# Columns 16 to 31 summed on VectorE and transposed by DMA; softmax sums of the later batches by accumulating transfers

## The chip, the cores and the metric

The kernel runs on one core of a Trainium2 chip. The metric is the device time in microseconds (us) of one execution. A core has five engines that run their own instruction streams in order: TensorE (PE, matrix products, with PEld for its weight loads), VectorE (DVE), ScalarE (ACT), GpSimd (POOL) and SyncE (SP). The last two mainly issue DMA transfers here. An instruction that has to wait holds up whatever stands behind it in the stream of its engine; between engines only semaphores order the work.

## The reference

Two stages. The first is a dynamic convolution: each position s of a batch has, for each of H = 8 heads, K = 7 weights, normalised by a softmax, which weigh the last 7 positions of x (D = 192 channels, 24 to a head). The second is a two-layer network whose hidden layer takes the maximum of two products.

```python
w = exp(weight_gen - max(weight_gen));  w = w / sum(w)        # [8, 4160, 8, 7], over the 7 taps
out[b,s,h,:] = sum over k of w[b,s,h,k] * x_padded[b, s+k, h, :]
y = out.reshape(33280, 192)
result = maximum(y @ w1, y @ w2) @ w_out                      # w1, w2: 192x1024, w_out: 1024x192
```

## The kernel before, in words

**Tiling.** The 33280 positions lie 260 to a partition on 128 partitions. One "column" is one position on every partition. Columns are taken in 17 batches: 16 of 16 columns and one of 4 (`BATCHES`, L50). `pieces` (L54) cuts a batch into units that are multiplied and summed at once: four units of 4 columns in batches 0 and 1, two of 8 columns in batches 2 to 15, one of 4 in the last. I write (b, o) for the unit of batch b that begins at its column o. PE works through 260 tiles, one a column's worth of hidden layer, in groups: 8 groups of two tiles (tiles 0 to 15), then groups of three (`GROUPS`, L71). Tiles 16 to 31 are batch 1, tile 32 begins batch 2.

**The softmax of a batch.** `load_wg` loads its weights (POOL queue). ACT takes the exponential (`exp_sum`, L131), DVE sums over the 7 taps (`red`, L143), ACT takes the logarithm (`ln`, L149), DVE subtracts it from the raw weights (`shift`, L153, in three pieces), and ACT takes the exponential of that, doubled and reordered by tap, as bf16 weights `en_t` (`weights`, L159), one call for each unit.

**The convolution.** DVE multiplies the unit's x by `en_t` for all seven taps into `m_t` (`mul`, L173), then adds the taps in three instructions (`adds`, L188: 3 pairs, 2 pairs, the last one into `y_t`). `transpose` (L212) issues a transposing DMA on SP's queue from `y_t` to `yt`, and then puts on POOL a "gate": a one-element copy that reads `yt` (L224) and so waits for the transfer. Behind the gate on POOL stand the next loads of x, a copy of six columns from one x tile to the next (`load_halo`, L123), and, for a unit at o = 0, the weights of batch b + 3.

**Batches 0 and 1 are different.** PE itself adds the taps there: `sum_transpose` (L239) multiplies `m_t` by an identity, accumulating over the taps, which sums and transposes in one, and ACT copies the result to `yt` (L255). In batch 0 DVE adds nothing. In batch 1 DVE makes the first of the three adds for the units at 4, 8 and 12 (`adds(..., True)`), so that four "taps" are left (`LEFT`); for the unit at 0 PE adds all seven.

**The network.** For each tile `hid_tile` (L291) makes the hidden products in PSUM, with w2 - w1 in place of both; ACT applies a relu (`relu`, L306); `out_first` and `out_second` (L345, L361) multiply by `w_out` and add the w1 part by a product with w1 @ w_out made once. ACT copies the output from PSUM (`evac`, L377), and SP stores it. A group with output columns has a relay on ACT (`relay`, L370) between the two halves of its output products, so PE waits there for ACT.

**Order.** All orders are written out by hand (`manual_schedule`). `hidden` (L458) makes one group: hidden products, output products of earlier columns, relus, the relay, the output copy. Up to group 7 the softmax and DVE steps stand explicitly in the code (L561 to L719: `rest_of_1`, `end_of_1`, and the table `early` with what goes into groups 3 to 7). From tile 16 on the table `due` (L721) says at which tile a softmax step of batch c is put into ACT's and DVE's order, and `extra` (L748) places `mul`, `adds` and `transpose` of the batches ahead: at tile 0 of batch b stands `mul(b + 1, 0)`, at tile 8 `mul(b + 1, 8)`, and the subtraction of batch b + 2 and the reduction of batch b + 3 run between the adds. `behind` (L262) gives a load one more thing to wait for, so that it takes its place among the transfers. How many columns of output each group takes (`OUTS`, L426) follows from which tiles are complete at its start, up to 4.

Of the kernel before, what the change touches and what calls it, by code (L numbers as in the profile page):

```python
# [9 lines left out]
FP32 = mybir.dt.float32  # L10
BF16 = mybir.dt.bfloat16
I32 = mybir.dt.int32
AF = mybir.ActivationFunctionType
# [10 lines left out]
def kernel(  # L24
# [9 lines left out]
    nc = tc.nc  # L34
# [19 lines left out]
    def pieces(b):  # L54
        n = BATCHES[b][1]
        at, done = [], 0
        for w in (4, 4, 4, 4) if b < 2 else (8, 8) if n == 16 else (n,):
            at.append((done, w))
            done += w
        return at  # L60
# [70 lines left out]
    def exp_sum(b, i=0, of=1):  # L131
        if i == 0:
            e_ts[b] = pe_.tile([P, BATCHES[b][1] * WGC], FP32, name="e_t", tag="e")
        w = BATCHES[b][1] * WGC // of
        nc.scalar.activation(out=e_ts[b][:, i * w:(i + 1) * w], in_=wg_ts[b][:, i * w:(i + 1) * w], func=AF.Exp)  # L135

# [6 lines left out]
    def red(b, i=0, of=1):  # L143
        if i == 0:
            s_ts[b] = psm.tile([P, BATCHES[b][1] * H], FP32, name="sum_t", tag="sum")
        hs, at, ap = part(b, i, of)
        nc.vector.reduce_sum(out=s_ts[b][:, hs], in_=_sub(e_ts[b], at, ap), axis=AX.X)  # L147

    def ln(b, i=0, of=1):  # L149
        s_t = s_ts[b][:, part(b, i, of)[0]]  # L150
        nc.scalar.activation(out=s_t, in_=s_t, func=AF.Ln)
# [7 lines left out]
    def weights(b, o):  # L159

        w = dict(pieces(b))[o]
        if b not in en_ts:
            en_ts[b] = pen.tile([P, 16 * WGC * 2], BF16, name="en_t", tag="en")
        J = 2 if w == 4 and b < 2 else 1
        N = w * H // J
        for j in range(J):
            nc.scalar.activation(  # L167
                out=_sub(en_ts[b], (o * WGC + j * N * K) * 2, [[2 * N, K], [2, N], [1, 2]]),
                in_=_sub(wg_ts[b], (o * H + j * N) * K, [[1, K], [K, N], [0, 2]]), func=AF.Exp,
            )  # L170


    def mul(b, o):  # L173

        n = dict(pieces(b))[o]
        if n == 4 and b < 2:
            m_out = _sub(m_t, K * o * D, [[64, 2], [P, K * 6], [1, 64]])
            x_in = _sub(xb_ts[b], o * D, [[2 * D, 2], [D, K], [1, 2 * D]])
        else:
            m_out = m_t[:, K * o * D:K * (o + n) * D]  # L180
            x_in = _sub(xb_ts[b], o * D, [[D, K], [1, n * D]])
# [6 lines left out]
    def adds(b, o, first=False, beside=lambda i, of: None):  # L188
# [10 lines left out]
        if first:  # L199
            return  # L200
# [11 lines left out]
    def transpose(u):  # L212
# [17 lines left out]
        if o == 0 and b + 3 < NB:  # L230
            load_wg(b + 3, nc.gpsimd)
# [5 lines left out]
    LEFT = (0, 1, 2, K - 1)  # L237

    def sum_transpose(u, taps=range(K)):  # L239
# [4 lines left out]
        for k in range(6):  # L244
            for t in taps:
                for r in range(2):
# [4 lines left out]
                        start=(k == 0 and t == taps[0]), stop=(t == taps[-1]),  # L251
# [260 lines left out]
    with tc.tile_pool(name="pstage", bufs=1) as pstage:  # L512
# [173 lines left out]
        weights(1, 4)  # L686
        mul(1, 4)
        relu(rd, 7, 1)
        exp_sum(2)
        red(2)  # L690
        adds(1, 4, True)
# [7 lines left out]
    def rest_of_1():  # L699
        mul(1, 8)  # L700

    def end_of_1():
        shift(2)
        adds(1, 8, True)
        mul(1, 12)
        exp_sum(3)
        red(3)
        adds(1, 12, True)


    none = lambda: None
    early = {
        3: (none, rest_of_1),
        4: (lambda: (behind(relu_of[8], load_x(2, 0, 8, halo=False)), sum_transpose(4),
                     behind(yt_of[4], load_wg(4, nc.gpsimd))), end_of_1),
        5: (lambda: sum_transpose(5, LEFT), none),
        6: (lambda: (behind(relu_of[12], load_x(2, 8, 8)), weights(2, 8), ln(3), sum_transpose(6, LEFT)), none),
        7: (lambda: (behind(relu_of[14], load_x(3, 0, 8)), sum_transpose(7, LEFT)), none),
# [3 lines left out]
    for c in range(3, NB):  # L722
        soon = c < 8
        parts_ = [(16 * (c - 2) + (8 if soon else 10 if c < NB - 1 else 15), True, lambda c=c: weights(c, 0))]
        if 8 in dict(pieces(c)):
            parts_.append((16 * (c - 2) + (14 if soon else 15), True, lambda c=c: weights(c, 8)))
        if c > 3:
            ln_at = -2 if c == 4 else 0 if c < 8 else 2 if c < 11 else 4
            parts_.append((16 * (c - 2) + ln_at, False, lambda c=c: ln(c)))
            parts_.append((16 * (c - 3) + (4 if c < 8 else 7), True, lambda c=c: exp_sum(c)))  # L730
# [17 lines left out]
    def extra(t):  # L748
# [7 lines left out]
        later = 0 if b < 4 else 5  # L756
        if s == later and b + 1 < NB:

            c = b + 1
            adds(c, 0, beside=lambda i, of: shift(c + 1, i, of) if c + 1 < NB else None)  # L760
        if s == 8 and b + 2 < NB:
            mul(b + 1, 8)
        if s == 8 + later and b + 2 < NB:
            adds(b + 1, 8, beside=lambda i, of: red(b + 3, i, 2) if b + 3 < NB and i < 2 else None)
        if k == n // 4 - 1 and 7 < u + 1 < NU:
            transpose(u + 1)

# [11 lines left out]
    early[3][1]()  # L779
    for g in range(4, len(GROUPS)):  # L780
# [3 lines left out]
        if g in early:  # L784
            hidden(g, OUTS[g], early[g][0], ahead=lambda: {4: lambda: (weights(1, 12), ln(2)), 5: lambda: weights(2, 0)}.get(g, none)())
            early[g][1]()
            steps(g, tiles)
# [32 lines left out]
```

## Time and profile before

| | |
|---|---|
| runs | 413.61, 412.78, 410.75 us; median 412.78 |
| span of the profiled execution | 409.1 us, first to last instruction (no other time of that execution is given) |
| granted TensorE clock, mean | 0.997 |
| PE, DVE, ACT, POOL busy | 97%, 92%, 87%, 17% of the span |
| DMA moved | 65.68 MB, mean 161 GB/s |
| `mul`, 8 columns (L182) | 28 instructions, mean 5751 ns |
| `adds`, 8 columns (L198, L204, L207) | 28 each, mean 2551, 1751 and 955 ns |
| sums over taps (L147), half a batch | 26 instructions, mean 614 ns |
| PE's partial sums (L248) | 564 matmuls, 9.8 us busy |
| gate copy (L224) | 29, mean 1171 ns |

How to read it: the page counts an engine as busy while an instruction of it runs. Successive instructions of DVE and ACT overlap by 0.05 to 0.15 us, so that what an instruction costs its engine is the distance from its start to the next start, a little under its duration. In a row of a timeline the columns are start, length, engine, line, operation, output and inputs; a bracket at the end gives the idle time of the engine before it and what ended that. In a row of a group they are the count, busy time, mean duration in ns, and the idle time before them.

### The profile page before, as it was taken

The page shows a single profiled execution, that of the slowest core. Times are in us where ns is not written, and L with a number is a line of the kernel's source. Part 1 is how long each engine was busy: PE and PEld are TensorE (multiplying, and loading weights), DVE is VectorE, ACT ScalarE, POOL GpSimd, SP SyncE. Part 2 cuts the span into 40 slices and gives each one's busy share as a digit, 9 for nine tenths or more (in the row PEclk, how much of TensorE's full clock was granted, in tenths as well). Part 3 has the DMA queues.
Part 4 walks back from the last instruction along what each step waited for, and adds up shares of the span by engine and source line. Part 5 has one row for each costly group of instructions (what it writes and reads, how often), then busy time and mean ns, then how long its engine had stood idle before and what let it go on. Part 6 is the DMA issues. An engine that isn't in the chain of part 4 may idle for free.

```text
span 409.1 us, 15992 instructions
## 1 busy us (share of the span) xinstructions
PE 398.8 (97%) x7350; PEld 317.1 (78%) x7350; DVE 374.4 (92%) x219; ACT 357.4 (87%) x424; POOL 68.7 (17%) x101
## 2 busy tenths in 40 slices
PE   7999999999999999999999999999999999999995
PEld 2688999677777777777777777777787777787795
DVE  6999999999999999999999999999999999999000
ACT  6899989999999988999988999988999989888771
POOL 0321101222211021221101221210122212210000
PEclk9999999999999999999999999999999999999998
DMA  8966667658657874963796497489648648744513
GB/s 245 250 152 164 116 151 186 143 143 184 150 97 219 217 118 99 260 176 74 224 195 146 96 251 180 82 195 238 120 106 241 166 64 244 151 89 79 213 61 136
DMA packets 60384, 65.68 MB, mean 161 GB/s; under 512 B 47615, under 2 KB 48511, under 8 KB 60318
## 3 DMA queue, kind: packets, MB, share of 16 engines
q1 hardware_dynamic: 51934, 40.54, 36.0%
q0 software_dynamic: 8240, 24.04, 29.5%
q8 instruction: 57, 0.93, 0.9%
q10 hardware_dynamic: 144, 0.10, 0.1%
q14 instruction: 9, 0.07, 0.1%
HBM read 35.96 MB, written 25.56 MB: 150 GB/s over the span
## 4 chain that ended last, share of the span: by engine, by line
DVE 73%; PE 17%; issue 4%; DMA 4%; SPq 0%; DVEq 0%; ACT 0%
DVE m_t L182 37%; DVE m_t L198 15%; DVE m_t L204 10%; PE op_ps L339 9%; PE hd L299 7%; DVE sum_t L147 3%; DVE y_t L207 3%; DVE wg_t L156 3%; DMA xs<-in_x_dram 3%; PE op_ps L351 2%; DMA yt<-y_t 1%; DVE wd L582 0%; DVE xb_t L618 0%; SPq L521 0%; SPq L104 0%
## 5 line engine op out<-in xcount | busy, mean ns | idle before, releaser
L309 ACT ACTIVATE rd_t<-hd 128x1024 bf16<-128x1024 f32 (+1 forms) x206 | 234.6, 1189 | 28.0 <-PE hd L299 26.5
L339 PE MATMUL op_ps<-wo,rd_t 64*128 64x192 bf16 x4160 | 210.6, 243 | 0.1
L339 PEld LDWEIGHTS <-rd_t 64*128 64x128 bf16 x4160 | 180.8, 94 | 15.7 <-ACTq L372 0.3
L299 PE MATMUL hd<-yt,wd 64*128 64x512 bf16 (+1 forms) x1584 | 187.3, 360 | 1.4 <-ACT rd_t L309 1.2
L182 DVE TENSOR_TENSOR m_t<-xb_t,en_t 128x10752 bf16<-128x10752 bf16 (+1 forms) x37 | 187.4, 5071 | 0.2
L299 PEld LDWEIGHTS <-wd 64*128 64x128 bf16 x1776 | 94.1, 94 | 43.3 <-issue 3.3
L224 POOL CAST gate<-yt 128x1 f32<-128x1 bf16 x29 | 34.0, 1171 | 275.7 <-DMA yt<-y_t 275.7
L198 DVE TENSOR_TENSOR m_t<-m_t 128x4608 bf16<-128x4608 bf16 (+1 forms) x32 | 76.8, 2401 | 0.1
L395 ACT COPY o_t<-op_ps 128x384 f32<-128x384 f32 (+1 forms) x99 | 57.3, 591 | 13.4 <-PE op_ps L339 13.3
L351 PE MATMUL op_ps<-w,yt 64*128 64x192 bf16 x780 | 55.5, 243 | 1.1 <-ACT o_t L395 1.0
L351 PEld LDWEIGHTS <-yt 64*128 64x128 bf16 x780 | 38.4, 94 | 17.5 <-issue 2.1
L204 DVE TENSOR_TENSOR m_t<-m_t 128x3072 bf16<-128x3072 bf16 (+1 forms) x29 | 50.0, 1724 | 0.1
L167 ACT ACTIVATE en_t<-wg_t 128x896 bf16<-128x896 f32 (+2 forms) x45 | 35.3, 820 | 0.0
L207 DVE TENSOR_TENSOR y_t<-m_t 128x1536 bf16<-128x1536 bf16 (+1 forms) x29 | 27.3, 941 | 0.5
L385 DVE COPY o_last<-op_ps 128x192 f32<-128x192 f32 x1 | 0.4, 358 | 25.9 <-ACT o_last L385 25.9
L156 DVE TENSOR_TENSOR wg_t<-wg_t,sum_t 128x280 f32<-128x280 f32 (+5 forms) x46 | 22.0, 481 | 0.0
L147 DVE TENSOR_REDUCE sum_t<-e_t 128x64 f32<-128x448 f32 (+2 forms) x31 | 19.6, 636 | 2.6 <-ACT e_t L135 2.6
L114 POOL DMA_DIRECT2D xb_t<-in_x_dram x33 | 17.7, 535 | 23.3 <-ACT rd_t L309 11.8
L135 ACT ACTIVATE e_t<-wg_t 128x896 f32<-128x896 f32 (+2 forms) x18 | 16.1, 899 | 2.5 <-DMA wg_t<-in_weight_gen_dram 2.5
L309 ACT ACTIVATE rd_t<-hdp 128x1024 bf16<-128x1024 f32 x16 | 16.2, 1048 | 0.6 <-PE hdp L299 0.6
L613 PE MATMUL warm<-ident 128*128 128x512 bf16 x38 | 11.0, 457 | 2.6 <-DVE ident L560 2.6
L299 PE MATMUL hdp<-yt,wd 64*128 64x256 bf16 x192 | 12.9, 269 | 0.1
(46 smaller groups left out, 73.6 us busy)
## 6 DMA issues: line engine op xcount, KB each, us to landing
out_dram<-o_t SPq DMA_DIRECT2D x28, 768.0 KB, 5.0
xb_t<-in_x_dram POOLq DMA_DIRECT2D x30, 384.0 KB, 5.2
wg_t<-in_weight_gen_dram POOLq DMA_DIRECT2D x14, 448.0 KB, 5.2
xb_t<-xb_t POOLq DMA_DIRECT2D x16, 288.0 KB, 5.2
out_dram<-o_t SPq DMA_DIRECT2D x8, 384.0 KB, 2.9
wg_t<-in_weight_gen_dram SPq DMA_DIRECT2D x2, 448.0 KB, 4.5
xs<-in_x_dram SPq DMA_DIRECT2D x2, 384.0 KB, 6.0
xb_t<-in_x_dram POOLq DMA_DIRECT2D x3, 192.0 KB, 5.1
```

What stands on the lines that cost most here:

```text
L156: nc.vector.tensor_tensor(out=w_t, in0=w_t, in1=_sub(s_ts[b], hs.start, [[1, hs.stop - hs.start], [0, K]]), op=ALU.subtract)
L167: nc.scalar.activation(out=_sub(en_ts[b], (o * WGC + j * N * K) * 2, [[2 * N, K], [2, N], [1, 2]]), in_=_sub(wg_ts[b], (o * H + j * N) * K ...
L182: return nc.vector.tensor_tensor(out=m_out, in0=x_in, in1=_sub(en_ts[b], o * WGC * 2, [[2, K * n * H], [0, G // 2], [1, 2]]), op=ALU.mult,)
L198: nc.vector.tensor_tensor(out=taps(0, 1, 3), in0=taps(0, 1, 3), in1=taps(3, 1, 3), op=ALU.add)
L204: nc.vector.tensor_tensor(out=taps(0, 2, 2), in0=taps(0, 2, 2), in1=taps(1, 5, 2), op=ALU.add)
L207: nc.vector.tensor_tensor(out=_sub(y_ts[b], o * D, [[64, 2], [P, 3 * w // 2], [1, 64]]), in0=taps(0, 1, 1), in1=taps(2, 1, 1), op=ALU.add,)
L224: nc.gpsimd.tensor_copy(out=gate, in_=yt[:, 0:1])
L299: nc.tensor.matmul(hid_out(t, f, j), lhsT=wd_at(j, s, f // 4, f % 4 * P, P), rhs=_sub(yt_ts[u][half(j), :], (s + j) % 3 * P, [[3 * P, w // ...
L309: relu_of[t0] = nc.scalar.activation(out=rd[:, k * 1024:(k + n) * 1024], in_=hd[:, at:at + n * 1024], func=AF.Relu)
L339: return nc.tensor.matmul(op_out(c), lhsT=rd[half(r), k * 1024 + at:k * 1024 + at + P], rhs=wo[half(r), f * D:(f + 1) * D], start=False, s ...
L351: nc.tensor.matmul(op_out(c + j), lhsT=yt_ts[u][half(j), (3 * i + (s + j) % 3) * P:(3 * i + (s + j) % 3 + 1) * P], rhs=w10[half(j), s * D: ...
L395: nc.scalar.copy(out=_sub(o, c % 24 * D, [[D, len(qs)], [h * D, 2], [1, D]]), in_=_sub(tile_, at + (qs[0] - p) * D, [[D, len(qs)], [512, 2 ...
```

## The change

1. Batch 1 is cut into two units of 8 columns as the later batches are. DVE makes all three adds for them and the transposing DMA moves the result; PE's partial sums of batch 1, ACT's copies of them and `LEFT` go. In the order this puts `mul(1, 0)`, `adds(1, 0)` and the transfer of unit 4, (1, 0), before group 5, and `adds(1, 8)` behind group 4.
2. For batches 3 to 15 (`by_dma`) the exponential is written in seven planes, one a tap, and three accumulating DMAs on POOL's queue add them: planes 3 to 5 onto 0 to 2, then two onto two, then one onto one. Each must wait for the one before. ACT takes the logarithm from plane 0. DVE's reductions for these batches go. One accumulate is placed behind each gate; batch 3 has its three in a row behind group 4, batch 4 its three in a row behind the gate of unit 5.
3. The subtraction goes in six pieces over both halves' adds (`shifts`), in place of three.
4. The due tiles of the softmax steps move, and the weights of a batch are loaded behind the gate of batch b - 4 instead of b - 3. The weights of batch 4 are loaded in group 5's place, their exponential stands behind group 7.

As group 4 starts when only four units of batch 0 are ready in the new cut, it gets no output columns, and the groups after it take up its two, until from group 18 on the distribution is as before.

```diff
@@ pieces
-        for w in (4, 4, 4, 4) if b < 2 else (8, 8) if n == 16 else (n,):
+        for w in (4, 4, 4, 4) if b == 0 else (8, 8) if n == 16 else (n,):
@@ exp_sum, red, ln
+        if by_dma(b):
+            N = BATCHES[b][1] * H
+            nc.scalar.activation(out=_sub(e_ts[b], 0, [[1, N], [N, K]]), in_=_sub(wg_ts[b], 0, [[K, N], [1, K]]),
+                                 func=AF.Exp)
+            return
...
+    def by_dma(b):
+        return 3 <= b < NB - 1
+
+    def add_planes(b, step):
+        if not by_dma(b):
+            return
+        N, e_t = BATCHES[b][1] * H, e_ts[b]
+        to, frm = (((0, [[1, 3 * N]]), (3 * N, [[1, 3 * N]])),
+                   ((0, [[N, 2], [1, N]]), (2 * N, [[4 * N, 2], [1, N]])),
+                   ((0, [[1, N]]), (N, [[1, N]])))[step]
+        nc.gpsimd.dma_start(out=_sub(e_t, *to), in_=_sub(e_t, *frm), accum_op=ALU.add)
...
     def red(b, i=0, of=1):
+        if by_dma(b):
+            return
...
     def ln(b, i=0, of=1):
+        if by_dma(b):
+            N = BATCHES[b][1] * H
+            s_ts[b] = psm.tile([P, N], FP32, name="sum_t", tag="sum")
+            nc.scalar.activation(out=s_ts[b], in_=e_ts[b][:, 0:N], func=AF.Ln)
+            return
@@ transpose, behind the gate
-        if o == 0 and b + 3 < NB:
-            load_wg(b + 3, nc.gpsimd)
+        if o == 0 and b + 4 < NB:
+            load_wg(b + 4, nc.gpsimd)
+        if o == 0 and b + 2 > 4:
+            add_planes(b + 2, 2)
+        if o == 8 and b + 3 > 4:
+            add_planes(b + 3, 1)
+        if u == 5:
+            for i in range(3):
+                add_planes(4, i)
@@ the first groups
-        weights(1, 4)
-        mul(1, 4)
         relu(rd, 7, 1)
         exp_sum(2)
-        red(2)
-        adds(1, 4, True)
+        adds(1, 0, beside=lambda i, of: red(2, i, 2) if i < 2 else None)
         sum_transpose(3)
         weights(1, 8)
...
+    def after_4():
+        exp_sum(3)
+        for i in range(3):
+            add_planes(3, i)
+        transpose(4)
+        adds(1, 8, beside=lambda i, of: shift(2, i, 2) if i < 2 else None)
+
     early = {
...
+        4: (lambda: behind(relu_of[8], load_x(2, 0, 8, halo=False)), lambda: ln(2), after_4),
+        5: (lambda: behind(relu_of[10], load_wg(4, nc.gpsimd)), lambda: None, lambda: None),
+        7: (lambda: None, lambda: None, lambda: exp_sum(4)),
     }
@@ due tiles
+    for c in range(2, NB):
+        t0 = 16 * (c - 2)
+        if c == 2:
+            parts_ = [(16, True, lambda: weights(2, 0)), (20, True, lambda: weights(2, 8))]
+        else:
+            parts_ = [(t0 + (11 if c < NB - 1 else 15), True, lambda c=c: weights(c, 0)),
+                      (t0 + 3, False, lambda c=c: ln(c))]
+            if 8 in dict(pieces(c)):
+                parts_.append((t0 + 20, True, lambda c=c: weights(c, 8)))
+        if c > 4:
+            parts_.append((t0 - 22 if by_dma(c) else t0 - 14, True, lambda c=c: (exp_sum(c), add_planes(c, 0))))
@@ extra
+        if s == 5 and b + 1 < NB:
+            adds(b + 1, 0, beside=lambda i, of: shifts(b + 2, i))
...
+        if s == 13 and b + 2 < NB:
+            adds(b + 1, 8, beside=lambda i, of: (shifts(b + 2, 3 + i) if by_dma(b + 2) else None,
+                                                 red(b + 3, i, 2) if b + 3 < NB and i < 2 else None))
```

More of the change, by code (lines that the diff above doesn't have):

```diff
@@ L163, in weights @@
             en_ts[b] = pen.tile([P, 16 * WGC * 2], BF16, name="en_t", tag="en")
-        J = 2 if w == 4 and b < 2 else 1
+        J = 2 if b == 0 else 1
         N = w * H // J
@@ L175, in mul @@
         n = dict(pieces(b))[o]
-        if n == 4 and b < 2:
+        if b == 0:
             m_out = _sub(m_t, K * o * D, [[64, 2], [P, K * 6], [1, 64]])
@@ L186, in mul, with adds @@
         )
-    def adds(b, o, first=False, beside=lambda i, of: None):
+    def adds(b, o, beside=lambda i, of: None):
         w = dict(pieces(b))[o]
@@ L198, in adds @@
         nc.vector.tensor_tensor(out=taps(0, 1, 3), in0=taps(0, 1, 3), in1=taps(3, 1, 3), op=ALU.add)
-        if first:
-            return
         beside(1, 3)
@@ L229, in transpose, with sum_transpose @@
             load_x(c, 8, BATCHES[c][1] - 8)
-        if o == 0 and b + 3 < NB:
-            load_wg(b + 3, nc.gpsimd)
+        if o == 0 and b + 4 < NB:
[7 more added lines that the diff above has]
+                add_planes(4, i)
     def half(j):
         return slice(64 * j, 64 * j + 64)
-    LEFT = (0, 1, 2, K - 1)
-    def sum_transpose(u, taps=range(K)):
+    def sum_transpose(u):
         b, o, n = UNITS[u]
@@ L244, in sum_transpose @@
         for k in range(6):
-            for t in taps:
+            for t in range(K):
                 for r in range(2):
@@ L250, in sum_transpose @@
                         lhsT=m_t[half(r), at:at + P], rhs=ident[half(r), half(r)],
-                        start=(k == 0 and t == taps[0]), stop=(t == taps[-1]),
+                        start=(k == 0 and t == 0), stop=(t == K - 1),
                         skip_group_check=True,
@@ L696 @@
     o_t.append(pout.tile([P, 24 * D], FP32, name="o_t", tag="o"))
[L699 to L705, printed above, removed]
+    def after_4():
         exp_sum(3)
-        red(3)
-        adds(1, 12, True)
-    none = lambda: None
+        for i in range(3):
+            add_planes(3, i)
+        transpose(4)
+        adds(1, 8, beside=lambda i, of: shift(2, i, 2) if i < 2 else None)
     early = {
[L713 to L718, printed above, removed]
+        4: (lambda: behind(relu_of[8], load_x(2, 0, 8, halo=False)), lambda: ln(2), after_4),
+        5: (lambda: behind(relu_of[10], load_wg(4, nc.gpsimd)), lambda: None, lambda: None),
+        7: (lambda: None, lambda: None, lambda: exp_sum(4)),
     }
     due = {}
[L722 to L730, printed above, removed]
+    for c in range(2, NB):
[9 more added lines that the diff above has]
+            parts_.append((t0 - 22 if by_dma(c) else t0 - 14, True, lambda c=c: (exp_sum(c), add_planes(c, 0))))
         for t, *step in parts_:
@@ L755, in extra, with shifts @@
             mul(b + 1, 0)
[L756 to L760, printed above, removed]
+        if s == 5 and b + 1 < NB:
+            adds(b + 1, 0, beside=lambda i, of: shifts(b + 2, i))
         if s == 8 and b + 2 < NB:
             mul(b + 1, 8)
-        if s == 8 + later and b + 2 < NB:
-            adds(b + 1, 8, beside=lambda i, of: red(b + 3, i, 2) if b + 3 < NB and i < 2 else None)
-        if k == n // 4 - 1 and 7 < u + 1 < NU:
+        if s == 13 and b + 2 < NB:
+            adds(b + 1, 8, beside=lambda i, of: (shifts(b + 2, 3 + i) if by_dma(b + 2) else None,
+                                                 red(b + 3, i, 2) if b + 3 < NB and i < 2 else None))
+        if k == n // 4 - 1 and u + 1 < NU:
             transpose(u + 1)
+    def shifts(c, i):
+        if c < NB:
+            shift(c, i, 6 if by_dma(c) else 3)
     def steps(g, tiles):
@@ L778 @@
     evac(OUTS[3][0] // 2, len(OUTS[3]) // 2)
-    early[3][1]()
+    mul(1, 8)
     for g in range(4, len(GROUPS)):
@@ L784 @@
         if g in early:
-            hidden(g, OUTS[g], early[g][0], ahead=lambda: {4: lambda: (weights(1, 12), ln(2)), 5: lambda: weights(2, 0)}.get(g, none)())
-            early[g][1]()
-            steps(g, tiles)
+            between, ahead, after = early[g]
+            hidden(g, OUTS[g], between, ahead=ahead)
+            after()
         else:
```

## The prediction

> **What bounds the kernel now.** I read the busy shares first, then the chain that ended last, the list of waits, and then the timelines of single engines around columns 16 to 31. Page, parts 1 and 4:
>
> ```profile
> PE 398.8 (97%) x7350; PEld 317.1 (78%) x7350; DVE 374.4 (92%) x219; ACT 357.4 (87%) x424; POOL 68.7 (17%) x101
> ...
> DVE 73%; PE 17%; issue 4%; DMA 4%; SPq 0%; DVEq 0%; ACT 0%
> ```
>
> The chain puts 73% on DVE, and that is easily misread. The waits say what it would be worth (engine and line, whom it waited for, us in total, times, longest):
>
> ```profile
> POOL gate L224 <- DMA yt<-y_t: 275.7, 29, 13.8
> ACT rd_t L309 <- PE hd L299: 26.5, 53, 0.8
> PE hd L299 <- ACT rd_t L309: 1.2, 5, 0.3
> PE hd L299 <- DMA yt<-y_t: 0.2, 1, 0.2
> ```
>
> PE waited for DVE's product once, for 0.2 us, while ACT waited for PE 53 times. PE's own timeline shows where:
>
> ```profile
> 47.43 1.49 PE L299 MATMUL hd<-yt,wd 64*128 64x256 bf16 x24 [0.19 <-ACT rd_t L309]
> ...
> 333.50 0.82 PE L299 MATMUL hd<-yt,wd 64*128 64x512 bf16 x6 [0.20 <-DMA yt<-y_t]
> ```
>
> PE begins columns 16 on (tile 16) at 47.43 and is never idle for long again; at 333.50 the transposed tile came just in time. From tile 32 (68.9) to tile 256 (390.8) PE takes 11.50 us per 8 columns. DVE takes 11.83 (its y_t writes L207 end at 55.9 and, 23 units of 8 columns on, at 328.1). So PE is the bound, with DVE's reserve eaten up only near the end: the transposed columns 32 on landed at 61.6, 7.3 us before PE took them. Less DVE work alone can return 0.2 us; less PE work up to what it weighs, if DVE keeps up; and any idle time of PE is lost.
>
> **Part 1, the sums of batches 3 to 15 leave DVE.** Columns are in batches of 16; (b, o) is column o of batch b. Rows by form:
>
> ```profile
> L147 DVE TENSOR_REDUCE sum_t<-e_t 128x64 f32<-128x448 f32 x26 | 15.9, 614 | 2.6 <-ACT e_t L135 2.6
> L156 DVE TENSOR_TENSOR wg_t<-wg_t,sum_t 128x280 f32<-128x280 f32 x26 | 11.5, 443 | 0.0
> L156 DVE TENSOR_TENSOR wg_t<-wg_t,sum_t 128x336 f32<-128x336 f32 x13 | 6.5, 501 | 0.0
> ```
>
> From start to start the two reductions of a batch cost 2 x 0.53. The subtraction goes from three pieces (0.36 + 0.36 + 0.42) to six, of 112 and 168 elements: a 112-element one lasts 0.27, and on the line through 280 and 336 one of 168 some 0.33, less 0.08 overlap 2 x 0.19 + 4 x 0.25 = 1.38. DVE's batch falls by 1.06 - 0.24 = 0.82 us, from 23.66 to 22.84, or 11.42 a unit: just under PE's 11.50. On the path this alone is worth 0.2. Its exponentials and Ln stay on ACT at their prices (0.98 and 0.34); the plane order is the order in which L167 reads, at 1.06 against 0.98.
>
> **Part 2, columns 16 to 31 leave PE.** Their partial sums on PE (L248) were 84 + 3 x 48 matmuls, by start distances 1.23 + 3 x 0.70 = 3.3 us between 34.1 and 47.1, and four ACT copies (L255) of 0.8. DVE gets two full sets of adds (2 x 5.1) for three first adds (3 x 1.27), +6.4, but no batch-3 reduction (-1.0).
>
> **Part 3, the new waits, on POOL and ACT.** The changed order on POOL is: load of x (2,0); three accumulating transfers of batch 3, each waiting for the one before; the gate copy on the transposed (1,0); x (2,8); weights of batch 5; weights of batch 4. And ACT has the exponential of batch 4 ahead of the relus of tile 16. So an ACT instruction on which PE hangs waits for a load that sits behind a gate on DVE's work. Before, that load went out at 36.9 and its exponential came at 55.6. How a gate and its loads run:
>
> ```profile
> 61.68 0.18 POOL L224 CAST gate<-yt 128x1 f32<-128x1 bf16 x1 [13.84 <-DMA yt<-y_t]
> 61.80 0.53 POOL L114 DMA_DIRECT2D xb_t<-in_x_dram  x1
> 62.32 0.55 POOL L104 DMA_DIRECT2D wg_t<-in_weight_gen_dram  x1
> ```
>
> and from the list of DMA issues (count, KB each, median us from issue to landing):
>
> ```profile
> xb_t<-in_x_dram POOLq DMA_DIRECT2D x30, 384.0 KB, 5.2
> wg_t<-in_weight_gen_dram POOLq DMA_DIRECT2D x14, 448.0 KB, 5.2
> xb_t<-xb_t POOLq DMA_DIRECT2D x16, 288.0 KB, 5.2
> ```
>
> DVE: product (1,0) starts at 25.7 as before (second of the three at 22.86), 5.67, then reductions of batch 2 and adds 6.2: y at 37.6; SP's transpose lands 3.6 to 5.4 after issue (median 3.9): 41.5, at worst 43.1. (1,8) ends at 49.4.
> ACT: relus 8 and 9 end by 34.7 as before; Ln of batch 2 must wait for the second reduction, now between the adds (end 35.0): 35.3; exponential of batch 3 ends 36.2. Then PE and ACT hand tiles 10 to 15 to and fro (relu pitch 0.95, output copy 0.4, no copies of L255): ACT is through tile 15 at about 44.5.
> POOL: the first accumulate goes at 36.2. What one takes no row shows. Lower end 2.5 us, a lone tile-to-tile copy of 288 KB (the one issued at 30.06); upper end 8.8, the worst weights load. I take 3.0, nearest to the lone copy: step one moves 192 KB, with nothing else on the queue, but reads its target too. The third is issued at 42.2, the gate is reached at 42.8, behind the landed transpose. Gate copy 1.17 (mean of 29), three issues: the batch-4 load goes at 45.0. A load behind one other takes 5.2; with 1.1 between landings and 0.5 between issues a second load ahead adds 0.6: 50.8. ACT has then stood 6.3 us.
> After that: exponential 0.85, three relus 2.72, copy 0.36, weights of (2,0) 1.06: 55.8. DVE was ready at 49.4 and has idled 6.4. It ends y (2,0) at 55.8 + 11.4 = 67.2, landed 0.3 + 3.9 later: 71.4. By PE's side alone tile 19 starts at 54.2 instead of 51.0.
>
> **Sum.** PE takes tile 32 at 71.4 instead of 68.9: +2.5. The output order gives group 4 no columns, so 22 are out instead of 26 there; at 1.57 us for two that is 3.1 still to do. 409.1 + 2.5 + 3.1 = 414.7 (by tile 19: 409.1 + 3.2 + 1.6 = 413.9; the later decides). The 3.3 us of PE's sums are inside this, as PE reaches tile 16 earlier. From there PE's 11.50 against DVE's 11.42 holds, with the 3.1 of output work becoming DVE's lead. The median of the runs is 412.8, 3.7 over this profiled span (no other time of that execution is given), and I carry that: 418.4.
>
> **Later batches.** 13 batches make 39 accumulates; at 0.55 us of POOL's time each they fit in the 275.7 us it waits for transposes. The last of a batch is issued behind its gate, x and weights, so it lands some 8.5 to 9 us after the transpose; ACT's Ln comes 5 to 7 us after PE starts that batch. With the lead of 3 that is covered; without it ACT waits, up to 3 us once, until the lead is there. I take 0 and keep 3 for the range. The steps that move in the due table cost the same on ACT; the weights of a batch's second half come some 5 or 6 tiles later (7 to 9 us), but DVE takes them 10 us or more after that, while that lead lasts. The load of the next weights goes one batch earlier, behind the same gates, into the buffer whose last reader, the weights of (b, 8), has run 12 tiles before: 0. The accumulates' 0.4 MB a batch beside DMA engines 60 to 80% busy I price at 0, with 1 to 2 us for late transposes as upper end; a gain there is excluded, since traffic is only added.
>
> **A rule against it.** POOL's DMA issues last 0.53 to 0.55 us (L104, L114, L127) beside a DVE that is busy 22.97 of 23.00 us between 70 and 93: no sign of blocking. The Trainium skill, "SBUF — State Buffer", section "A bandwidth-pool intuition that's wrong (but worth ruling out)", tells of POOL-issued transfers taking about 3100 ns instead of 620 beside a blocking DVE copy; by it three accumulates would be 7.4 us later and the sum about 425. Its section "Who interferes with whom" exempts two-input operations, as nearly all of DVE's here are. The same skill's "DMA: Bandwidth & Descriptors", section "Anatomy of one DMA", gives 2.0 us plus bytes over 436 GB/s: an estimate of 2.5 us for step one, by which the gate is reached at 41.8 and the sum is 417.4.
>
> **Rivals.** (1) Not slower: no stall at tile 16. The place is ACT's exponential of batch 4. If its weights land by 44.5, DVE goes on at 49.7, tile 32 at 65.3: 409.1 - 3.6 + 3.1 = 408.6, with 3.7: 412.3. Every us of landing after 44.5 costs one. For it: weights loads alone landed in 3.6. Against: the gate, earliest 41.5 by the transpose alone, and three loads. (2) Faster: DVE is the bound after all, as the chain says: 13 x 0.82 = 10.7 less, 5.4 more for columns 16 to 31: 403.8, or 407.5. Against: 0.2 us of waiting. (3) Slow accumulates, 6 us: gate at 48.8, everything 6 later, 424.4, and with 3 us of ACT's Ln 427.4. For it: the median of 5.2 under load.
>
> **How the numbers follow.** About 1%, 4 us, is what a measurement can tell from no change. Forecast 0.56, 415.5 to 421 for itself (landing of the transpose 3.6 to 5.4, accumulates 2.5 to 5); no stall or a short one 0.22; slow accumulates 0.16; DVE-bound 0.06. Slower by over 1% (above 416.9): 0.50 + 0.16 = 0.66; within 1%: 0.06 + 0.22 = 0.28; faster 0.06. Range 412 to 426: it leaves out the DVE case 0.06, a tail of the no-stall case and one of the slow accumulates, together under 0.2.
>
> **What would show it.** In the changed profile: ACT idle some 6 us ahead of the batch-4 exponential, released by a weights load; DVE idle 6 us ahead of the product (2,0); PE idle around tile 18; no DVE idle later; units of 11.4 on DVE and 11.5 on PE. I am wrong if ACT does not stand there, if accumulates take over 5 us, or if Ln waits recur in each batch.

## The result and the profile after

The kernel after took 486.08 us (median of 4 runs, 483.69 to 488.09), the kernel before on the same chip 411.92 (4 runs): a ratio of 1.179, with a 95% interval of 1.173 to 1.184. The forecast was 418.4 us in a range of 412 to 426. The direction was right and the size was not: 74 us were lost where some 6 were expected. In the experiments below, single runs of e5, e6, e7 and e14 (465.21, 1401.52, 430.13 and 416.81 us), which stand apart from the other runs of their kernel, are left out of medians and ratios; with them the medians are 424.68, 435.43, 424.67 and 411.68, the figures that later expectations use.

The profiled execution after took 483.69 us; its span is 481.8. Its page, parts 1 (busy time), 2 (busy tenths in 40 slices) and 4 (the chain that ended last):

```profile
PE 410.0 (85%) x7026; PEld 316.3 (66%) x7026; DVE 370.3 (77%) x236; ACT 365.1 (76%) x412; POOL 187.9 (39%) x142
...
PE   7988299919998937999895699999579998999995
...
DVE  6999199967994949889396897969599795999300
...
PE 30%; DMA 20%; issue 18%; DVE 12%; POOL 9%; ACT 8%; SPq 0%; POOLq 0%; ACTq 0%
```

PE fell from 97% busy to 85%, DVE from 92% to 77%, and POOL rose from 68.7 to 187.9 us. No engine is busy nearly throughout any more, and in the chain, transfers have 20% and POOL 9%, where before transfers had 4% and POOL no share. The slices (12 us each) show holes that come back every four to seven slices, not one stop at the start. PE's own starts divide the 72.7 us that the span grew: tile 32 began at 79.00 (before 68.93), 10.1 later; from there to tile 256 it took 383.8 (before 321.9), 61.9 more; the tail after that is 0.8 longer. So the loss that I forecast, at tile 16, is there at a larger size, and six times as much lies in the batches that I had priced at zero.

The list of waits (engine and line, whom it waited for, us in total, times, longest) of the kernel after:

```profile
POOL e_t L154 <- ACT e_t L136: 69.1, 8, 13.1
DVE wg_t L182 <- ACT sum_t L174: 54.8, 11, 7.4
...
PE op_ps L380 <- ACT o_t L424: 44.4, 11, 9.9
...
ACT sum_t L174 <- DMA e_t<-e_t: 35.4, 6, 10.2
```

Read from the bottom: ACT's logarithm (L174) waits for an accumulating transfer, DVE's subtraction (L182) for the logarithm, PE (L380) for ACT. The groups show what stands ahead of those transfers on POOL (the first number is busy time, the second the mean in ns, and the last the idle time before). The first line is the gate of the kernel before, the others are of the kernel after:

```profile
L224 POOL CAST gate<-yt 128x1 f32<-128x1 bf16 x29 | 34.0, 1171 | 275.7 <-DMA yt<-y_t 275.7
...
L248 POOL CAST gate<-yt 128x1 f32<-128x1 bf16 x31 | 118.1, 3810 | 128.4 <-DMA yt<-y_t 128.4
...
L154 POOL DMA_DIRECT2D e_t<-e_t x39 | 40.2, 1070 | 90.4 <-ACT e_t L136 69.1
...
L136 ACT ACTIVATE e_t<-wg_t 128x896 f32<-128x896 f32 x13 | 23.5, 1806 | 20.7 <-DMA wg_t<-in_weight_gen_dram 20.3
```

The gate copy, 128 elements, took 1.17 us in the mean before and takes 3.81 now, 84 us more in all. The mean hides that seven of them take over 11. One such stretch, in three cuts of the timelines of POOL, DVE and ACT (start, duration, instruction, in brackets the idle time before it and what ended it):

```profile
131.88 11.98 POOL L248 CAST gate<-yt 128x1 f32<-128x1 bf16 x1 [10.54 <-DMA yt<-y_t]
...
144.91 1.84 POOL L154 DMA_DIRECT2D e_t<-e_t  x2
```

```profile
132.40 0.27 DVE L182 TENSOR_TENSOR wg_t<-wg_t,sum_t 128x112 f32<-128x112 f32 x1
...
138.07 5.75 DVE L208 TENSOR_TENSOR m_t<-xb_t,en_t 128x10752 bf16<-128x10752 bf16 x1
151.22 0.28 DVE L182 TENSOR_TENSOR wg_t<-wg_t,sum_t 128x112 f32<-128x112 f32 x1 [7.40 <-ACT sum_t L174]
```

```profile
150.88 0.31 ACT L174 ACTIVATE sum_t<-e_t 128x128 f32<-128x128 f32 x1 [2.90 <-DMA e_t<-e_t]
```

The copy's transposed tile has landed at 131.88, but the copy does not end before 143.86; in between, DVE passes seven ends of its instructions. That is 0.04 us after DVE's product of 138.07 to 143.82, the moment at which DVE stops for lack of a logarithm. The accumulating transfer is issued behind the copy, at 144.91, the logarithm runs when it has landed, and DVE goes on at 151.22. It is a circle: DVE keeps the copy out as long as it has work, and it runs out of work because what it needs stands behind the copy. A second way round the same circle is a weights load behind a held copy: the copy of 80.50 lasts 14.82, the load goes at 95.81, and ACT and then PE stand (cuts of the timelines of POOL, ACT and PE):

```profile
80.50 14.82 POOL L248 CAST gate<-yt 128x1 f32<-128x1 bf16 x1
...
95.81 0.58 POOL L104 DMA_DIRECT2D wg_t<-in_weight_gen_dram  x1
```

```profile
103.45 1.76 ACT L136 ACTIVATE e_t<-wg_t 128x896 f32<-128x896 f32 x1 [9.62 <-DMA wg_t<-in_weight_gen_dram]
```

```profile
106.86 0.66 PE L380 MATMUL op_ps<-w,yt 64*128 64x192 bf16 x6 [9.86 <-ACT o_t L424]
```

### The profile page after: what moved, and what is told of

Same layout as the page of the kernel before. It is cut to its first block, busy times and chain, and to the rows that moved or that the text cites. A ratio compares the mean times of both kernels' runs of the same rounds, so it can differ in the third digit from the quotient of the medians.

```text
span 481.8 us, 15394 instructions
## 1 busy us (share of the span) xinstructions
PE 410.0 (85%) x7026; PEld 316.3 (66%) x7026; DVE 370.3 (77%) x236; ACT 365.1 (76%) x412; POOL 187.9 (39%) x142
## 4 chain that ended last, share of the span: by engine, by line
PE 30%; DMA 20%; issue 18%; DVE 12%; POOL 9%; ACT 8%; SPq 0%; POOLq 0%; ACTq 0%
PE op_ps L368 13%; PE hd L328 12%; DMA e_t<-e_t 9%; POOL gate L248 6%; ACT rd_t L338 4%; DMA wg_t<-in_weight_gen_dram 4%; DMA yt<-y_t 4%; DVE m_t L224 4%; DVE m_t L208 4%; DMA xb_t<-in_x_dram 3%; PE op_ps L380 3%; DVE m_t L228 2%; PE warm L642 2%; POOL e_t L154 2%; DVE y_t L231 1%
## 5 line engine op out<-in xcount | busy, mean ns | idle before, releaser
L368 PE MATMUL op_ps<-wo,rd_t 64*128 64x192 bf16 x4160 | 216.3, 247 | 8.9 <-ACTq L401 8.8
L368 PEld LDWEIGHTS <-rd_t 64*128 64x128 bf16 x4160 | 185.8, 96 | 27.9 <-ACTq L401 11.0
L328 PE MATMUL hd<-yt,wd 64*128 64x512 bf16 (+1 forms) x1488 | 192.3, 381 | 7.2 <-ACT rd_t L338 7.1
L248 POOL CAST gate<-yt 128x1 f32<-128x1 bf16 x31 | 118.1, 3810 | 128.4 <-DMA yt<-y_t 128.4
L380 PE MATMUL op_ps<-w,yt 64*128 64x192 bf16 x780 | 56.6, 247 | 45.8 <-ACT o_t L424 44.4
L380 PEld LDWEIGHTS <-yt 64*128 64x128 bf16 x780 | 38.8, 95 | 66.0 <-issue 51.5
L154 POOL DMA_DIRECT2D e_t<-e_t x39 | 40.2, 1070 | 90.4 <-ACT e_t L136 69.1
L182 DVE TENSOR_TENSOR wg_t<-wg_t,sum_t 128x168 f32<-128x168 f32 (+4 forms) x86 | 28.0, 327 | 54.8 <-ACT sum_t L174 54.8
L136 ACT ACTIVATE e_t<-wg_t 128x896 f32<-128x896 f32 x13 | 23.5, 1806 | 20.7 <-DMA wg_t<-in_weight_gen_dram 20.3
L193 ACT ACTIVATE en_t<-wg_t 128x896 bf16<-128x896 f32 (+2 forms) x39 | 33.9, 886 | 0.0
L174 ACT ACTIVATE sum_t<-e_t 128x128 f32<-128x128 f32 x13 | 4.1, 319 | 38.4 <-DMA e_t<-e_t 35.4
L114 POOL DMA_DIRECT2D xb_t<-in_x_dram x33 | 23.0, 698 | 15.6 <-DVE m_t L208 10.8
L127 POOL DMA_DIRECT2D xb_t<-xb_t x16 | 8.8, 548 | 22.9 <-DMA xb_t<-in_x_dram 22.9
```

Of the source, the lines that this page charges most:

```text
L154: nc.gpsimd.dma_start(out=_sub(e_t, *to), in_=_sub(e_t, *frm), accum_op=ALU.add)
L193: nc.scalar.activation(out=_sub(en_ts[b], (o * WGC + j * N * K) * 2, [[2 * N, K], [2, N], [1, 2]]), in_=_sub(wg_ts[b], (o * H + j * N) * K ...
L248: nc.gpsimd.tensor_copy(out=gate, in_=yt[:, 0:1])
L328: nc.tensor.matmul(hid_out(t, f, j), lhsT=wd_at(j, s, f // 4, f % 4 * P, P), rhs=_sub(yt_ts[u][half(j), :], (s + j) % 3 * P, [[3 * P, w // ...
L368: return nc.tensor.matmul(op_out(c), lhsT=rd[half(r), k * 1024 + at:k * 1024 + at + P], rhs=wo[half(r), f * D:(f + 1) * D], start=False, s ...
L380: nc.tensor.matmul(op_out(c + j), lhsT=yt_ts[u][half(j), (3 * i + (s + j) % 3) * P:(3 * i + (s + j) % 3 + 1) * P], rhs=w10[half(j), s * D: ...
```

## The experiments

Fifteen kernels, each compared with runs of the kernel before on the same chip (411.1 to 412.3 us). Theory A: the gate copies, held up by DVE, make the loss. Theory B: the accumulating transfers themselves do, by their landing times or their POOL time. Differences between two kernels are known to some 1 to 3 us.

**e1, the gate without a read.** The gate becomes a memset that waits for the same transpose.

```diff
-        nc.sync.dma_start_transpose(
+        moved = nc.sync.dma_start_transpose(
...
-        nc.gpsimd.tensor_copy(out=gate, in_=yt[:, 0:1])
+        behind(moved, nc.gpsimd.memset(gate, 0.0))
```

> The changed kernel with each gate on POOL made a memset that waits for the transposing DMA itself, so that it writes but does not read a tile. Theory A (the gate copy, which reads, gets through only at some of DVE's instruction boundaries, up to 15 us late since DVE's reductions are gone, and the accumulates and loads behind it are late with it): the long gates go, Ln's waits for accumulates fall from 35 to under 8 us in total, and what is left is the stop at tile 16, 415 to 428 us. Theory B (POOL's waits for the exponentials, 69 us in all, and the accumulate chains hold the queue, the gate copy is only where it shows): the gates stay late, 465 us or more.

Measured: 429.15 us, ratio 1.043 [1.040, 1.046]: 57 us of the 74 are gone with this one instruction. Group and waits of e1:

```profile
L248 POOL MEMSET gate<- 128x1 f32 x31 | 5.1, 165 | 207.5 <-DMA yt<-y_t 207.5
```

```profile
POOL e_t L154 <- ACT e_t L136: 55.4, 8, 12.4
...
ACT e_t L136 <- DMA wg_t<-in_weight_gen_dram: 10.0, 1, 10.0
DVE wg_t L182 <- ACT sum_t L174: 10.0, 4, 3.3
```

No gate is held; DVE's waiting for logarithms falls from 54.8 to 10.0. POOL still waits 55.4 us for ACT's exponentials (69.1 after), so that large number never was the loss: it is idle time of an engine that is not late. The longest wait that stays on ACT is the stop at the start (10.0).

**e2, the same gate in the kernel before.** The two lines of e1's edit, made there.

> The kernel before with the same memset gates. Theory A: the gate copies there last at most 1.87 us and nothing on the path stands behind them, so no difference within 0.7 per cent. Theory B: the same. A gain of over 1 per cent would mean that the copies already cost something before.

411.11 us, ratio 0.999 [0.998, 1.001]. Before, the copies cost nothing that shows: the longest took 1.87 us. That nothing urgent stood behind them either is read from the order and was not tested.

**e3, the columns alone.** The sums go back to DVE, with three pieces to a shift.

```diff
     def by_dma(b):
-        return 3 <= b < NB - 1
+        return False
...
         adds(1, 8, beside=lambda i, of: shift(2, i, 2) if i < 2 else None)
+        red(3)
```

> The changed kernel without the accumulating transfers: all batches are summed by DVE's reductions in the old layout, with three subtractions a batch; batch 1 stays cut in two units, summed on DVE, and the due tiles are the changed ones. Theory A: reductions are back between the multiplies, no gate copy lasts over 3 us, ACT stops some 6 us ahead of tile 16, and DVE's 11.83 us a unit against PE's 11.5 from a lead of nothing adds 7 more: 420 to 430 us. Theory B says the same of this run. A third theory, that the cut of batch 1 or the new due tiles cost most of the 74 us: 460 us or more.

422.83 us, ratio 1.027 [1.025, 1.030]. The gate copies take 1453 ns in the mean, none over 1.9 us. So the columns, with the new due tiles and the late load that this run keeps, cost 11 us, and they are not what holds the copies.

**e4, the fifth load early.** The load of batch 4's weights leaves the place behind the gate.

```diff
     def after_4():
         exp_sum(3)
+        load_wg(4, nc.gpsimd)
         for i in range(3):
             add_planes(3, i)
...
-        5: (lambda: behind(relu_of[10], load_wg(4, nc.gpsimd)), lambda: None, lambda: None),
+        5: (lambda: None, lambda: None, lambda: None),
```

> The changed kernel with the weights of batch 4 loaded ahead of batch 3's accumulates instead of behind the gate of (1, 0). Both theories: ACT's 10.7 us stop ahead of tile 16 goes; if it is a cost of its own, 8 to 11 us less than the changed kernel, 474 to 478; if the later waits take over its time, less than 3 us off, 483 or more.

479.83 us, ratio 1.168 [1.163, 1.172]: 6.3 us less (known to some 3), between the two expectations. **e5** joins the edits of e1 and e4:

> The changed kernel with the memset gates and with batch 4's weights loaded ahead of the accumulates of batch 3. If the stop at tile 16 and the blocked gate copies are all but ACT's dearer plane exponentials (1.81 us instead of 0.98, 13 times) and some waits of Ln: 429.2 less the 10 us stop, 417 to 421 us. If DVE's added work on columns 16 to 31 bounds the start anyway: 424 us or more.

424.40 us, ratio 1.031 [1.028, 1.034]. The load is worth 4.8 us here, not the 10.0 that ACT stood: with ACT's stop gone, tile 32 began at 71.91 (near the 71.4 of my forecast by coincidence, as that was reached with the stop), and PE waited 2.6 us for a transposed tile instead. The rest, some 13 us, has another cause, and it takes two runs below to name it.

**e6, three pieces, the copies kept.** Theory S: what holds the copy is that DVE's work beside the additions was cut into small pieces. The shift goes back to 280, 280 and 336 elements, all in the first unit; copies and accumulating transfers stay.

```diff
-            adds(b + 1, 8, beside=lambda i, of: (shifts(b + 2, 3 + i) if by_dma(b + 2) else None,
-                                                 red(b + 3, i, 2) if b + 3 < NB and i < 2 else None))
+            adds(b + 1, 8, beside=lambda i, of: red(b + 3, i, 2) if b + 3 < NB and i < 2 else None)
...
-            shift(c, i, 6 if by_dma(c) else 3)
+            shift(c, i, 3)
```

> The changed kernel with its gate copies kept, and the subtraction of batches 3 to 15 in three pieces of 280, 280 and 336 elements in the first unit, as before; the second unit's adds then follow the multiply directly. Theory S (pieces of 112 and 168 elements between DVE's instructions leave no opening for the copy, those of 280 do, and so does an add that waits for its multiply): every gate copy lasts under 3 us and the time is that of the memset gates, 425 to 433 us. Theory R (the openings were the reductions, which read one tile only): copies of over 8 us remain and the time stays above 460 us.

434.06 us, ratio 1.057 [1.053, 1.062]. The group of e6:

```profile
L248 POOL CAST gate<-yt 128x1 f32<-128x1 bf16 x31 | 38.5, 1243 | 194.9 <-DMA yt<-y_t 194.9
```

The longest copy takes 2.52 us. So, with the reductions gone, 52 us are lost by cutting DVE's subtractions into six: not by their own 0.2 us a batch, but because the copy no longer finds its moment. e6 is 5 us slower than e1, and the copies, 1.24 us each where a memset took 0.17, are a likely but untested cause: from tile 32 to tile 256 PE took 333.0 us in e6 and 329.9 in e1. **e7** is e6 with the early load of e4:

> Three pieces and the early load of batch 4's weights together, gate copies kept: as the memset gates with the early load, 416 to 422 us; DVE saves 0.24 us a batch more, which PE's bound hides.

424.39 us, ratio 1.032 [1.030, 1.034]: the time of e5. Its longest copy, 5.16 us, is one that came early in a product of DVE and went in at that product's end. What the copies cost is settled; the next four runs ask what about the pieces matters.

**e8, six pieces in the kernel before,** two behind one another at each of the three places.

```diff
-            adds(c, 0, beside=lambda i, of: shift(c + 1, i, of) if c + 1 < NB else None)
+            adds(c, 0, beside=lambda i, of: [shift(c + 1, 2 * i + j, 6) for j in range(2)] if c + 1 < NB - 1
+                 else shift(c + 1, i, of) if c + 1 < NB else None)
```

> The kernel before with the subtraction of each batch, still all in the first unit's adds, in six pieces of 112 and 168 elements, two at a time. Theory S: the gate copies that arrive during a first unit's multiply are held for 6 us and more, until a reduction of the next unit lets them in; what stands behind them has over 10 us in hand, so the time is within 1 per cent of before. Theory R: the copies get in at the end of the multiply as before, none over 2 us.

414.08 us, ratio 1.008 [1.006, 1.009], and no copy over 1.9 us. Theory S, as stated, falls: small pieces alone hold nothing. (I read the 0.75% as DVE's time for three more pieces a batch: from tile 184 to 224 the transposed tiles land 0.04 to 0.14 us before PE takes them, where before all but one, at 0.04, had 0.99 us or more.)

**e9, the six pieces of after in pairs.** Theory W: it is the length of the short work between two long instructions that counts.

```diff
...
-            shift(c, i, 6 if by_dma(c) else 3)
...
+            for p in ((0, 1), (2,), ())[i]:
+                shift(c, first + p, 6)
```

> The kernel after with its gate copies, accumulating transfers and six pieces per shift kept; only the places change: of each unit's three pieces the first two (112 and 168 wide, 0.27 and 0.33 us) stand one behind the other right after the multiplication and the third after the addition of three planes. Theory W: the held copy needs a stretch of fp32 work of some 0.4 us or more between two of VectorE's long bf16 instructions, since it went in at each multiplication's end followed by 280 (0.44 us) or by 112 and 168 (0.60 us), and at 2 of 9 followed by 112 alone. Then no gate copy is over 2.6 us, their mean is 1.2 to 1.4, and the time is 430 to 437 us, as with three pieces (435.43). Rival: six pieces with accumulating transfers on POOL hold the copy wherever the pieces stand: the longest over 8 us and the time over 455.

435.43 us, ratio 1.057 [1.053, 1.061]; copies 1160 ns in the mean, the longest 2.62:

```profile
L248 POOL CAST gate<-yt 128x1 f32<-128x1 bf16 x31 | 36.0, 1160 | 192.1 <-DMA yt<-y_t 192.1
```

Nothing was removed, no instruction added; two of each unit's three pieces moved by one place, and 51 us came back.

**e10, one small piece alone in the kernel before,** pieces of 112, of 168 + 168 and of 112 + 168 + 168.

```diff
-            adds(c, 0, beside=lambda i, of: shift(c + 1, i, of) if c + 1 < NB else None)
+            adds(c, 0, beside=lambda i, of: [shift(c + 1, j, 6) for j in ((0,), (1, 2), (3, 4, 5))[i]]
+                 if c + 1 < NB - 1 else shift(c + 1, i, of) if c + 1 < NB else None)
```

> The kernel before (no accumulating transfers, reductions on VectorE) with each shift of batches 3 on made in six pieces at its old three places: one piece of 112 alone after the multiplication, two (168, 168) after the addition of three planes, three (112, 168, 168) after the addition of two. Theory W (a stretch of fp32 work under 0.4 us does not let the waiting gate copy in): most of the 12 copies that wait at such a multiplication's end (before: 12 of 12 let in there) now go in only behind the addition of three planes, about 2.9 us later, so that the mean of the 31 goes from 1.17 to 1.8 to 2.3 us and the longest to 4 to 5; the time 411 to 415. Rival, that the accumulating transfers are needed for a held copy: mean 1.1 to 1.3, none over 1.9, the same time.

413.49 us, ratio 1.005 [1.003, 1.007], and the rival's picture: mean 1357 ns, none over 2.4 us. At each of the 12 ends of a product followed by 112 alone the copy got in. Theory W holds as "long enough work lets it in" and falls as "short work never does".

**e13, a wait on the piece.** Theory V: the short piece lets the copy in when it carries a semaphore wait. In the traces so far 13 of 15 such pieces of 112 ahead of an addition let it in, and 1 of 12 without a wait.

```diff
...
+            piece = shift(c, i, 6 if by_dma(c) else 3)
+            if i == 3:
+                behind(relu_of[max(k for k in relu_of if k <= at - 2)], piece)
```

> The kernel after with one thing more: the first of the second unit's three pieces (112 wide, after the multiplication) also waits for ScalarE's evacuation of a tile two before the one at which it is written, which is done long before. Nothing is moved and no instruction is added; only that piece carries a semaphore wait that is already met, as the first unit's piece does (for the logarithm). Theory V: whether a waiting gate copy gets in at a gap-free end of the multiplication goes with such a wait on the next short instruction: in the traces so far 13 of 15 copies got in at a 112 piece with a wait followed by an addition, 1 of 12 at one without. Then the copies that were held from the second unit's multiplication on (131.88, 161.31, 217.33, 331.68, 386.10 us in the trace after) go in at its end; the longest gate copy is under 5 us and the time 428 to 440 us. Rival (what the piece waits for is a coincidence; its place or POOL's accumulating transfers decide): copies over 10 us remain and the time is over 465.

485.16 us, ratio 1.181 [1.175, 1.187]: theory V falls. All pieces of 112 carry a wait now, and 4 of 11 let the copy in. Most long copies stand where they stood:

```profile
132.11 11.93 POOL L248 CAST gate<-yt 128x1 f32<-128x1 bf16 x1 [10.74 <-DMA yt<-y_t]
```

This is what all traces with gate copies give when the ends of DVE instructions are counted at which a copy was waiting and DVE went on without a gap (its rarer pairs left out; "in": the copy ended within 0.12 us of that end):

| DVE instruction that ended, and the next work | in | not in |
|---|---|---|
| product, then 280 or 448 elements (0.44 us or more) | 75 | 2 |
| product, then a reduction | 64 | 1 |
| product, then 112 + 168 behind one another (0.60 us) | 24 | 1 |
| addition of three planes, then 280, 448 or a reduction | 12 | 0 |
| product, then 112 alone, then an addition: e10 | 12 | 0 |
| the same: after, e4 and e13 | 6 | 20 |
| addition of three or of two planes, then 168 alone | 9 | 64 |
| last addition, then the next product | 0 | 22 |

The pairs left out are of the last batches: a product, then 56 elements alone (0.21 us), 11 in and 3 not; a product, then 112 and a short reduction, 0 in and 3 not. The six that were not in are of after, e4 and e13, and went in 0.17 to 0.23 us after the product.

Where work of 0.44 us or more, or a full reduction, follows a long bf16 instruction, the copy gets in nearly always (the four not in of the first three rows had begun at most 0.1 us before that end); where the next product follows directly, never. For one short piece behind a product the length does not decide it: 112 alone let the copy in 12 of 12 times in e10, and 56 alone 11 of 11 times outside after, e4 and e13, while in these three 112 alone let it in 6 of 26 times. What sets them apart stays open; e10 has reductions in its other unit, and no run parted that from the rest.

**e11 and e12, the remaining 13 us.** Both start from e7. e11 leaves the plane order out of the exponentials (so the sums are not the softmax sums), e12 leaves the accumulating transfers out (so the logarithm reads one plane of seven).

```diff
 e11
-            nc.scalar.activation(out=_sub(e_ts[b], 0, [[1, N], [N, K]]), in_=_sub(wg_ts[b], 0, [[K, N], [1, K]]),
-                                 func=AF.Exp)
+            nc.scalar.activation(out=e_ts[b][:, 0:K * N], in_=wg_ts[b][:, 0:K * N], func=AF.Exp)
 e12
-        if not by_dma(b):
-            return
+        return
```

> The kernel after with the shifts in three pieces and the fifth load early (424.67 us), but batches 3 on get their exponentials in the order of the loaded values instead of in planes, so that the sums that the transfers make are not the softmax sums (the output is not the reference's). It tells what the reading in planes costs: 1.81 us instead of 0.98 for 896 columns, 13 times, 10.8 us of ScalarE's time. Theory P (ScalarE's longer work delays the evacuations and weights that PE and VectorE wait for): 415 to 420 us. Rival (PE and VectorE are balanced to 0.04 us at the transposes and set the time): 423 to 425.

> The same kernel (424.67 us) with the 39 accumulating transfers left out, so that the logarithm reads one plane instead of the sum of seven (the output is not the reference's); the exponentials in planes stay. It tells what the transfers cost by themselves, 40.4 us of POOL's time in issues and their landing. If the rest of the loss (424.67 against 411.9) comes from POOL's issues and late logarithms: 415 to 420 us. If it comes from ScalarE's exponentials or from VectorE's longer path at the start: 422 to 425.

e11: 419.97 us, ratio 1.022 [1.018, 1.027]. e12: 418.78, 1.018 [1.016, 1.020]. (The expectation of e11 speaks of reading in planes; it is the writing that is in planes.) The exponential in e11, and the same line in e12:

```profile
L136 ACT ACTIVATE e_t<-wg_t 128x896 f32<-128x896 f32 x13 | 12.5, 958 | 0.5
```

```profile
L136 ACT ACTIVATE e_t<-wg_t 128x896 f32<-128x896 f32 x13 | 23.6, 1813 | 0.5
```

**e14, neither:** both edits.

> The kernel with three pieces and the early load (424.67 us) with both changes that were made singly: exponentials in the loaded order (419.97) and no accumulating transfers (418.78). The output is not the reference's. If the two costs lie on one path each and add, 4.7 and 5.9 us: 413 to 415.5 us, about the time before plus VectorE's longer start. If they hide each other or the start sets the rest: 417 to 420 us.

411.52 us, ratio 1.000 [0.998, 1.002]. Taken in one order, planes cost 4.4 and transfers 8.5; in the other, transfers 5.6 and planes 7.3. Together they are the whole 12.9 us, and singly 10.0, so that the two costs add roughly, within what the runs can tell. Summing batch 1 on DVE does not make the start longer by itself: tile 32 begins at 67.02 here, and at 68.93 before.

**e15, the columns with the early load,** reductions on DVE: the edits of e3 and e4.

> The columns alone (reductions on VectorE, no accumulating transfers; 422.83 us) with the fifth load early, nothing left out. Without sums of any kind and without reductions the same start gave 411.68. If the columns' own loss was the late load and the stop behind it (6.6 us in its trace): 415 to 418 us. If VectorE, which keeps its reductions and has lost its lead to the columns (the transposes landed 0.04 to 2 us before PE used them in the columns alone), sets the time anyway: 420 to 424 us.

418.98 us, ratio 1.015 [1.012, 1.017], between the expectations. The late load was 3.9 us of e3's loss; DVE's reductions, against e14, are 7.5.

So from after to before, one step at a time: 486.08, less 52.0 for the held copies (e6), less 9.7 for the late load (e7), less 4.4 for the planes (e11), less 8.5 for the transfers (e14): 411.5. In another order the shares differ, as e1, e4 and e5 show for the first two: the load alone is worth 6.3 us with the copies held and 4.8 with memsets. No version here is faster than the kernel before.

## Why the prediction was wrong, point by point

- **What bounds before (PE, DVE just behind).** Right as far as the runs reach: e8 and e10 add a little DVE time and cost 0.75% and 0.5%, with landings down to 0.04 us before PE.
- **Part 1.** DVE's unit came out as worked: from one y_t write to the next (82.98 to 94.33) 11.35 us against 11.42. "Its exponentials stay at their prices (0.98)" failed: 1.81 us each, 23.5 instead of 12.7 in all. I took the plane order's price from L167, but that line reads with a step of 7 and writes in order; the new one reads in order and writes with a step of 128 elements, and of that the trace had no row. In the time it is 4.4 to 7.3 us (e11, e14).
- **Part 2.** PE reached tile 16 at 44.38, as the working says (some 3 us before the old 47.43). It was not kept.
- **Part 3, the stop at tile 16.** Mechanism right, size too small: ACT stood 10.73 us, not 6.3. The terms, on POOL:

```profile
37.40 0.89 POOL L154 DMA_DIRECT2D e_t<-e_t  x1 [2.66 <-ACT e_t L136]
41.15 1.23 POOL L154 DMA_DIRECT2D e_t<-e_t  x1 [2.86 <-DMA e_t<-e_t]
45.97 0.90 POOL L154 DMA_DIRECT2D e_t<-e_t  x1 [3.59 <-DMA e_t<-e_t]
46.55 2.08 POOL L248 CAST gate<-yt 128x1 f32<-128x1 bf16 x1
```

```profile
55.44 1.73 ACT L136 ACTIVATE e_t<-wg_t 128x896 f32<-128x896 f32 x1 [10.73 <-DMA wg_t<-in_weight_gen_dram]
```

  The first issue came 1.2 later than worked (0.8 of it the longer exponential), from issue to issue 3.75 and 4.82 instead of 3.0 each, so the third went at 45.97 and not at 42.2; the copy took 2.08 instead of 1.17. Tile 19 came at 58.98 (54.2) and tile 32 at 79.00 (71.4). The sum lets DVE's side decide tile 32; here its transposed columns had landed at 77.2, and PE, late since tile 19, came to them 1.8 later.
- **Later batches: the failed step.** "I take 0 and keep 3 for the range." The 39 transfers' issues, 1.07 us each and not 0.55, did fit into POOL's waiting, but the gate ahead of them did not keep its 1.17 us: its mean was 3.81, the longest 14.82. I carried a mean of before into a DVE stream that I had just changed, in the same part that counted the six pieces, and asked what the pieces cost DVE (0.2 us a batch) but not who slips in between them. e6 and e9 show it: 52 and 51 us with the same transfers and gates. Also the "8.5 to 9 us after the transpose" for the last transfer was built on that gate. The transfers without held gates cost 5.6 to 8.5 us (e12, e14), not 0 to 3.
- **The rule weighed.** No issue on POOL stretched to 3100 ns (accumulating ones took up to 1.31 us, ordinary ones 0.53 to 0.59 and a few up to 2.2), and that judgement held. The sentence on "Who interferes with whom" holds for the issues that it speaks of, but it leaves out the other half of that rule. In the Trainium skill, "SBUF — State Buffer", that section exempts two-input VectorE instructions only against a GpSimd instruction that only writes SBUF; with one that reads SBUF, it says, they contend. The gate copy reads. The runs agree: the reading gate is held up to 14.82 us, the memset takes 165 ns (e1). This was the rule that spoke against the change, and I had weighed it for the issues alone and not for the gate.
- **Rivals.** None of the three had it. Two of the conditions under which I said I would be wrong were met: Ln waits came back (ACT's Ln waited for a transfer 6 times in 13 batches, DVE for Ln 11 times), and two of the three accumulating steps took over 5 us from issue to landing (medians 5.3, 4.5 and 5.4).

## What to carry to other kernels

A tiny instruction that stands as a gate in a queue can cost far more than its old mean when another engine's stream is changed (here 1.17 us in the mean before, up to 14.82 after), so price it by its longest wait and by what stands behind it. Where only an order is wanted, gate with an instruction that does not read (here a memset behind the same semaphore, 0.17 us). And when work is taken off a nearly balanced engine and given to others, add up what the others pay: 7.5 us of reductions saved (e15 against e14) were bought with 12.9 of strided exponentials and transfers.

## What the runs showed of the hardware

- A 128x1 POOL copy that reads SBUF waited up to 14.82 us beside back-to-back DVE instructions with two inputs, past 11 of their ends in that case and 7 in the stretch from 131.88; a POOL memset did not wait (165 ns). Which ends let it in is in the table above; only its rows with long work and with no work between are regular.
- An accumulating tile-to-tile transfer occupied POOL for 0.89 to 1.31 us per issue in the kernel after, an ordinary tile-to-tile copy (L127) 0.54 to 0.57.
- An fp32 exponential over 896 elements took 1.81 us when it read in order and wrote each element 128 behind the last, and 0.96 when it wrote in order too. One that reads with a step of 7 and writes 896 bf16 in order (L193) took 1.03.
- The granted TensorE clock was 0.941 over the span after and 0.997 before; in e7, with the copies let in, it was 1.000. After the hole of 9.86 us that ends at 106.86 in after, it was 0.52 from 107 to 111, where 45 matmuls ran, and 1.00 from 111 to 115, where 73 ran, PE being busy throughout both. By an estimate from these, 28 matmuls at 4/73 us, this hole cost some 1.5 us besides its own length.
